# Loading head 0's K tile ahead of the query weights in a one-token attention and MLP kernel

## The chip, the cores and the metric

The kernel runs on one core of one Trainium2 chip. The metric is device time in microseconds (us): the median of several executions. A profile's span, from its first to its last record, is about 1.8 us shorter than the time of the same execution. Times come with a state, fast or slow.

Five engines matter below: PE (matrix multiply; its weight loads are listed as PEld), DVE (vector), ACT (scalar), POOL, and SP, whose queue ("SPq" in the profile) issues almost all transfers from HBM to the on-chip memory. The letter q behind an engine's name means its instruction queue.

## The reference, cut to what matters

```python
xn = layernorm(x)                       # x: 4 x 1 x 576
# A: one-token attention over the last 2048 cache positions
q = (xn @ wq)                           # wq: 576 x 4096, 32 query heads of 128
k = k_cache[:, :, -2048:, :]            # 4 batches, 16 kv heads, 2 query heads each
v = v_cache[:, :, -2048:, :]
o = softmax(q k^T / sqrt(128)) v
a = o @ wo                              # wo: 4096 x 576
# B: a mixer and an MLP (one position, so the shifted mixer term is zero)
b = xn + gelu(layernorm(xn) @ w3) @ w4  # w3: 576 x 4608, w4: 4608 x 576
out = x + a + b
```

Each weight and each cache element in the window is used once. That makes 87 MB to read for very little arithmetic.

## The kernel before

All large loads go through the SP queue, in program order. There are six buffers for K and V tiles. A K tile (one kv head, all four batches, 2 MB) is turned by four DVE transposes, and its buffer is free after the fourth.

```python
NKV = 6
kvp = ctx.enter_context(tc.tile_pool(name="kv", bufs=NKV))
def load_kv(kind, h):
    t = kvp.tile([P, NC, Dh], BF16, tag="kv", ...)
    nc.sync.dma_start(out=t..., in_=win[:, h]...)
...
nc.scalar.dma_start(out=x_bf[:], in_=x2)
nc.sync.dma_start(out=wq_sb[:, 0:KJ * NQ], in_=wq_main)            # 4096 KB
nc.sync.dma_start(out=wq_sb[:, KJ * NQ:], in_=A_wq[KJ * P:D, :]...) #  512 KB
...                                     # constants, layernorms
...                                     # q = xn @ wq, q turned and spread into qz
order = [("K", 0), ("K", 1), ("K", 2)]
for h in range(Hkv):
    order.append(("V", h))
    if h + 3 < Hkv:
        order.append(("K", h + 3))
W3_AFTER = ("V", 2)
pos = {"n": 0, "free": NKV}
flush_loads()                           # as many loads as buffers are free
k_transpose(0, 0)
for t in range(Hkv):
    for s in range(NSL):                # NSL = 4 slices of a head
        ...
        k_transpose(next slice)         # DVE
        ...
        pv(t - 2, s)                    # PE: probabilities times V, two heads behind
        k_scores(t, s)                  # PE: qz times the transposed K
    pos["free"] += 1                    # K's buffer (and, from t = 2, a V buffer)
    flush_loads()
```

The `w` pool holds wq, then w3, then w4 in one place, so w3 can be loaded only after the query matmuls. Two further points matter. DVE works in program order, and the first K transpose stands behind the whole query chain. Transfers are issued in program order too, so an issue that has to wait holds back the ones behind it.

## Time and profile before

| | before |
|---|---|
| time, median of 3 | 211.92 us (211.91 to 212.02) |
| span of the profiled execution | 210.2 us |
| bytes moved | 87.32 MB |
| SP's transfer queue | 97.5% of 16 engines' span |
| PE, DVE busy | 70%, 57% |

The page of the kernel before, cut to the lines that show the limit. The rows of digits are busy tenths in 40 equal slices of the span, and "GB/s" is what the 16 DMA engines moved in each slice.

```profile
span 210.2 us, 2389 instructions
...
PE 147.2 (70%) x941; PEld 62.4 (30%) x955; DVE 120.1 (57%) x217; ACT 33.9 (16%) x64; POOL 2.8 (1%) x15
...
DMA  7999999999999999999999999999999999999991
GB/s 281 418 399 430 421 430 435 427 430 436 436 442 414 426 433 420 446 424 433 436 421 433 430 420 437 433 433 422 433 426 430 422 442 433 421 436 426 421 414 60
...
q1 hardware_dynamic: 6640, 87.17, 97.5%
```

The row of DMA digits has no hole between the first slice and the last. The Trainium skill, page "DMA: Bandwidth & Descriptors", section Specifications, gives 435 GB/s as the fabric ceiling. This trace sits at 414 to 446 from the fourth slice to the one before the last, 429 on average, so the queue is not only busy but near that rate.

The timeline of the start, with start and duration in us, engine, source line, operation, output<-input, and in brackets how long the engine had been idle and what ended that:

```profile
13.14 3.91 PE L285 MATMUL q_ps<-wq_sb,xnT 128*32 128x512 bf16 x40 [0.18 <-DMA wq_sb<-in_A_wq_dram]
...
21.36 4.62 DVE L225 STREAM_TRANSPOSE kt<-kn 128x1024 int32<-128x1024 int32 x4
...
26.01 0.54 SPq L103 DMA_DIRECT2D kn<-in_A_k_cache_dram  x1
...
32.01 0.54 SPq L103 DMA_DIRECT2D vn<-in_A_v_cache_dram  x1
...
37.85 0.62 PE L390 MATMUL O<-vn,PT 128*32 128x512 bf16 x4 [4.19 <-DMA vn<-in_A_v_cache_dram]
...
41.77 0.55 SPq L103 DMA_DIRECT2D kn<-in_A_k_cache_dram  x1
...
74.59 2.37 DVE L225 STREAM_TRANSPOSE kt<-kn 128x1024 int32<-128x1024 int32 x2 [10.78 <-DMA kn<-in_A_k_cache_dram]
```

Read it as follows. The query matmuls start when wq lands. The query chain takes 8.2 us, and then the first K transpose runs. At 26.01 head 0's transposes are done and K4 is issued into the freed buffer. At 37.85 PE has waited 4.19 us for V0, and at 74.59 DVE has waited 10.78 us for K5: compute is ahead of the transfers. In these traces an issue on this queue also waits for the landing of the transfer eight places before it: V1, the ninth, is issued at 13.11, when wq, the first, has landed, and V5, the twentieth, at 68.43, when w3, the twelfth, has.

The chain of waits (start, us, what) names the same start and then steps in units of landings:

```profile
0.73 12.36 DMA wq_sb<-in_A_wq_dram
...
32.59 35.77 DMA w_sb<-in_B_w_dram
68.43 33.13 DMA vn<-in_A_v_cache_dram
```

### The profile page before, as it was taken

How to read it: one execution, taken by the hardware profiler on the slowest of the kernel's cores; microseconds unless marked ns; L12 is line 12 of the kernel's file. 1: busy time of each engine (PE TensorE's matmuls, PEld its weight loads, DVE VectorE, ACT ScalarE, POOL GpSimd, SP SyncE). 2: the span in 40 equal slices, each digit the busy share in tenths (PEclk: the TensorE clock that was granted, in tenths of full speed). 3: DMA queues.
4: the chain of work that ended last, by engine and by line, in shares of the span. 5: the costliest groups of instructions: out<-in, count | busy, mean ns of one | idle time of the engine just before them, and what ended most of it. 6: DMA issues, size and time to landing. Idle time of an engine off the chain costs nothing.

```text
span 210.2 us, 2389 instructions
## 1 busy us (share of the span) xinstructions
PE 147.2 (70%) x941; PEld 62.4 (30%) x955; DVE 120.1 (57%) x217; ACT 33.9 (16%) x64; POOL 2.8 (1%) x15
## 2 busy tenths in 40 slices
PE   0395694789394008849699689997883956988954
PEld 0132231224131002314154234343431321543533
DVE  4832999267831082637603879898578381593220
ACT  7603100021111000202012211220211020202300
POOL 4010000000000000000000000000000000000000
PEclk9998599589979555979699969999999695899999
DMA  7999999999999999999999999999999999999991
GB/s 281 418 399 430 421 430 435 427 430 436 436 442 414 426 433 420 446 424 433 436 421 433 430 420 437 433 433 422 433 426 430 422 442 433 421 436 426 421 414 60
DMA packets 6659, 87.32 MB, mean 415 GB/s; under 512 B 748, under 2 KB 1016, under 8 KB 1400
## 3 DMA queue, kind: packets, MB, share of 16 engines
q1 hardware_dynamic: 6640, 87.17, 97.5%
q8 instruction: 7, 0.11, 0.2%
q14 instruction: 4, 0.03, 0.0%
q10 hardware_dynamic: 8, 0.00, 0.0%
HBM read 87.17 MB, written 0.00 MB: 415 GB/s over the span
## 4 chain that ended last, share of the span: by engine, by line
DMA 65%; PE 22%; DVE 8%; issue 2%; ACT 1%; SPq 1%; DVEq 0%
DMA w_sb<-in_B_w_dram 33%; DMA vn<-in_A_v_cache_dram 26%; PE S L338 9%; DMA wq_sb<-in_A_wq_dram 6%; DVE kt L225 4%; PE O L390 3%; PE g_ps L456 2%; PE acc L183 2%; PE q_ps L285 2%; PE oT L403 1%; DVE mx L344 1%; PE S L360 1%; DVE qz L317 1%; PE gT_ps L468 1%; ACT q_sb L296 1%
## 5 line engine op out<-in xcount | busy, mean ns | idle before, releaser
L225 DVE STREAM_TRANSPOSE kt<-kn 128x1024 int32<-128x1024 int32 x64 | 76.3, 1216 | 11.1 <-DMA kn<-in_A_k_cache_dram 10.8
L338 PE MATMUL S<-kt,qz 128*128 128x512 bf16 x242 | 76.1, 437 | 5.2 <-DVE kt L225 3.1
L390 PE MATMUL O<-vn,PT 128*32 128x512 bf16 x256 | 27.9, 434 | 38.7 <-DMA vn<-in_A_v_cache_dram 37.5
L338 PEld LDWEIGHTS <-qz 128*128 128x128 bf16 x256 | 21.8, 104 | 42.0 <-issue 26.2
L366 ACT ACTIVATE E<-S 128x512 bf16<-128x512 f32 x16 | 9.5, 597 | 119.8 <-PE S L360 119.8
L390 PEld LDWEIGHTS <-PT 128*32 128x32 bf16 x256 | 7.3, 95 | 47.0 <-DVE kt L225 25.2
L372 DVE STREAM_TRANSPOSE PT<-E 128x512 bf16<-128x512 bf16 x16 | 11.4, 710 | 15.1 <-ACT E L366 15.1
L356 DVE TENSOR_REDUCE nm<-mg 8x1 bf16<-8x16 f32 x16 | 2.3, 146 | 23.0 <-PE mg L351 22.9
L397 ACT ACTIVATE O_sb<-O,rd 128x512 f32<-128x512 f32 x16 | 11.0, 686 | 16.2 <-issue 11.0
L344 DVE TENSOR_REDUCE mx<-S 128x1 f32<-128x512 f32 x16 | 10.5, 657 | 1.3 <-PE S L338 1.3
L413 DVE TENSOR_REDUCE on<-oT 128x8 bf16<-128x128 f32 x16 | 4.5, 280 | 11.1 <-PE oT L403 11.1
L403 PE MATMUL oT<-ident_w,O_sb 128*128 128x128 f32 x64 | 10.6, 291 | 0.2 <-issue 0.2
L403 PEld LDWEIGHTS oT<-ident_w,O_sb 128*128 128x128 f32 x64 | 8.6, 153 | 4.6 <-issue 2.4
L183 PE MATMUL acc<-wo_sb,op 128*8 128x288 bf16 x56 | 7.5, 286 | 0.0
L376 PEld LDWEIGHTS dn<-rs,same_j 128*128 128x128 f32 x32 | 5.8, 188 | 2.9 <-ACT E L366 0.7
L360 PE MATMUL S<-nm,j_row 8*128 8x512 bf16 x16 | 6.6, 410 | 0.0
L183 PE MATMUL acc<-w_sb,gT 128*8 128x288 bf16 x38 | 5.1, 286 | 1.9 <-DMA w_sb<-in_B_w_dram 1.9
L329 PE MATMUL S<-negbig,ohT 4*128 4x512 bf16 x16 | 6.2, 385 | 0.2 <-issue 0.2
L351 PE MATMUL mg<-dm,sel_jb 128*8 128x16 bf16 x16 | 2.8, 174 | 4.0 <-DVE dm L346 3.5
L183 PEld LDWEIGHTS <-op 128*8 128x8 bf16 x64 | 4.6, 87 | 2.4 <-issue 0.3
L456 PE MATMUL g_ps<-w_sb,ln2T 128*32 128x512 bf16 (+1 forms) x50 | 5.3, 480 | 0.0
L351 PEld LDWEIGHTS <-sel_jb 128*8 128x8 bf16 x16 | 1.3, 83 | 12.7 <-issue 6.8
(93 smaller groups left out, 80.0 us busy)
## 6 DMA issues: line engine op xcount, KB each, us to landing
kn<-in_A_k_cache_dram SPq DMA_DIRECT2D x16, 2048.0 KB, 22.3
vn<-in_A_v_cache_dram SPq DMA_DIRECT2D x16, 2048.0 KB, 24.8
wo_sb<-in_A_wo_dram SPq DMA_DIRECT2D x4, 1152.0 KB, 25.5
w_sb<-in_B_w_dram SPq DMA_DIRECT2D x1, 4608.0 KB, 35.8
wq_sb<-in_A_wq_dram SPq DMA_DIRECT2D x1, 4096.0 KB, 12.4
w_sb<-in_B_w_dram SPq DMA_DIRECT2D x1, 1728.0 KB, 33.6
w_sb<-in_B_w_dram SPq DMA_DIRECT2D x1, 1440.0 KB, 27.8
w_sb<-in_B_w_dram SPq DMA_DIRECT2D x2, 576.0 KB, 33.8
```

What stands on the lines that cost most here:

```text
L183: nc.tensor.matmul(out=to[q:q + OR, :], lhsT=lhsT[:, NI - 1 - i:NI - 1 - i + OR], rhs=rhs[:, i * CW:(i + 1) * CW], start=start, stop=False ...
L225: nc.vector.transpose(out=kt[:], in_=src)
L329: nc.tensor.matmul(out=S_ps[h][:].rearrange("p (c k) -> p c k", k=QD), lhsT=ohT[:], rhs=negbig[:].unsqueeze(1).to_broadcast([B, SC, QD]), ...
L338: nc.tensor.matmul(out=S_ps[h][:], lhsT=qz[:, z0:z0 + P], rhs=kt[:, ib, :, e:2 * QD:2].rearrange("p c k -> p (c k)"), start=False, stop=Fa ...
L344: nc.vector.reduce_max(out=mx[:], in_=S_ps[h][:], axis=AX.X)
L360: nc.tensor.matmul(out=S_ps[h][:], lhsT=j_row[:], rhs=st.pop(("nm", h))[:, 0:1].to_broadcast([NJ, NW]), start=False, stop=False, skip_grou ...
L366: nc.scalar.activation(out=E[h][:].rearrange("p c k -> p (c k)"), in_=S_ps.pop(h)[:], func=ACT.Exp, scale=scale, accum_out=rs[:])
L372: nc.vector.transpose(out=PT[h][:], in_=E.pop(h)[:])
L390: nc.tensor.matmul(out=O_ps[h][g * QD:(g + 1) * QD], lhsT=PT[h][:, c, :], rhs=vn[:, :, c, :], start=(s == 0), stop=False, skip_group_check ...
L397: nc.scalar.activation(out=O_sb[h][:], in_=O_ps.pop(h)[:], func=ACT.Copy, scale=st.pop(("rd", h))[:, 0:1])
L403: nc.tensor.transpose(out=oT[:, s, :], in_=o[:, s, :], identity=ident_w[:, s * NJ:s * NJ + P])
L456: nc.tensor.matmul(out=g_ps[g * QD:(g + 1) * QD], lhsT=ln2T[:, k, :], rhs=rhs, start=(j == 0), stop=False, skip_group_check=True)
```

## The change

The query chain needs wq, and the attention needs K0 as well. The change puts K0 first on the sync queue and wq behind it. Nothing else moves.

```diff
     wq_main = A_wq[0:KJ * P, :].rearrange("(p j) n -> p (j n)", j=KJ)
+    load_kv("K", 0)
     nc.sync.dma_start(out=wq_sb[:, 0:KJ * NQ], in_=wq_main)
...
-    order = [("K", 0), ("K", 1), ("K", 2)]
+    order = [("K", 1), ("K", 2)]
...
-    pos = {"n": 0, "free": NKV}
+    pos = {"n": 0, "free": NKV - 1}
```

## The prediction

> **What bounds the kernel now.** The DMA queue. The page gives 87.32 MB in a span of 210.2 us, queue 1 busy 97.5% of 16 engines' span. In the view by windows of 5 us, the DMA share is 0.98 or more from 5 to 205 us except at 65 to 70 (0.86), with 405 to 466 GB/s elsewhere. The Trainium skill, "DMA: Bandwidth & Descriptors", section Specifications, puts the fabric ceiling at 435 GB/s; most windows read 423 to 436, so this trace agrees. Outside lie only the start (0 to 5: share 0.67) and the tail after the last w4 piece (205 to 210). PE is busy 70%, DVE 57%; both wait for loads, e.g. PE 37.5 us for V tiles and DVE 10.8 us once for K5.
>
> **What the change does.** No byte, transfer or instruction is added. K0 (2048 KB) moves from third to first, so wq (4608 KB in two transfers) lands 2.1 MB later: at about 425 GB/s, 4.9 us (estimate from the windows). The DVE program order stays: the first K transpose still follows the q chain. In the timeline wq's matmuls start at 13.14 when wq lands, and q to qz ends at 21.36, when the first K transpose starts; K0 has landed by then anyway. So K0's early arrival is useless, and the first 8.2 us chain starts later:
> - q matmuls 13.1 -> about 18.1; first K transpose 21.4 -> about 26.3.
> - K4's issue, which waits for head 0's last transpose (26.01), -> about 31.
> - V2's and w3's issues (32.01, 32.59) -> about 37.
> - V1's issue (13.11, waits for wq's landing) will instead wait for K0, -> about 6 to 7.
>
> **How much is critical.** Nearly none. By 13 us 18.5 MB are issued (wq, K0 to K2, wo, V0, K3, V1), and at 26 us some 7.5 MB or 17 us of them are still to move; five us later some 12 us. So the transfers never run dry. The delay is also absorbed in compute: at 37.85 PE had waited 4.19 us for V0, whose landing is unchanged because the bytes ahead of it are the same. After the change PE reaches that point at about 38, so this wait almost vanishes, and K5's issue (41.77) comes at 41.8 to 43. By K5's landing (74.6, after w3, DVE had idled 10.8 us) the two kernels must be back on the same schedule; the tail is identical.
>
> Expected: +0.1 us, within run noise (211.91 to 212.02 before). **211.9 us, 8 in 10 between 211.3 and 212.7.** Faster by over 2%: 0.01; within 2%: 0.97; slower by over 2%: 0.02.
>
> **What would show each step.**
> - wq matmuls start at 17.5 to 18.7 us; first K transpose at 25.7 to 27.
> - GB/s in slices 2 to 39 unchanged, queue 1 share 97 to 98%.
> - PE's wait for V0 at 38 us shrinks from 4.19 to under 1 us; the total of PE's V waits falls to about 33 us.
> - DVE's wait for K5 still ends at 74.6 us, give or take 0.5.
> - The last w4 piece lands within 0.5 us of 205.0.
>
> **What would make it wrong.** If the first transfer starts more slowly or quickly with K0 in front (window 0 to 5), the whole stream shifts by that, tenths of a us. If PE's granted clock (0.50 at 20 to 25, 0.63 to 0.68 at 35 to 45) falls lower after the shift, heads 1 to 4 catch up later, but time is lost only if the queue runs dry. A queue limit on outstanding transfers (V5's issue at 68.43 waited for w3's landing) could bite elsewhere.

## The result

| | before | after |
|---|---|---|
| time, median of 6 | 211.96 us (211.83 to 212.03) | 212.09 us (211.96 to 212.20) |
| span of the profiled execution | 210.2 us | 210.1 us |
| SP's transfer queue | 97.5% | 97.4% |

The ratio is 1.0006 (95% interval 0.9993 to 1.0019). Ratios here and below are the recorded ones: the mean time of one kernel's fast runs over that of the other's of the same rounds, so not quite the ratio of the medians quoted. Those of e3, e5 and e9 come out of the listed times only if the profiled execution is left out; this is said where it matters.

The page of the changed kernel:

```profile
span 210.1 us, 2403 instructions
...
DMA  6999999999999999999999999999999999999991
GB/s 247 452 399 430 418 437 430 432 418 443 433 449 408 423 440 418 446 421 440 434 418 437 430 415 436 434 437 426 427 432 430 417 438 440 424 427 431 423 413 70
...
q1 hardware_dynamic: 6640, 87.17, 97.4%
```

The first two slices exchange 34 GB/s: 281 and 418 before, 247 and 452 after, 699 in sum both times. From the third slice to the one before the last the two rows differ by at most 3%. (The other 14 "instructions" of the span line are matmul records: 941 before, 955 after. A few can be missing from a trace.)

The timeline of the changed kernel, the same events as before:

```profile
17.98 4.46 PE L286 MATMUL q_ps<-wq_sb,xnT 128*32 128x512 bf16 x40 [4.93 <-DMA wq_sb<-in_A_wq_dram]
...
26.54 4.62 DVE L226 STREAM_TRANSPOSE kt<-kn 128x1024 int32<-128x1024 int32 x4
...
31.19 0.54 SPq L103 DMA_DIRECT2D kn<-in_A_k_cache_dram  x1
...
37.67 0.54 SPq L103 DMA_DIRECT2D vn<-in_A_v_cache_dram  x1
...
39.26 0.40 PE L391 MATMUL O<-vn,PT 128*32 128x512 bf16 x4
...
43.92 0.54 SPq L103 DMA_DIRECT2D kn<-in_A_k_cache_dram  x1
...
74.50 2.37 DVE L226 STREAM_TRANSPOSE kt<-kn 128x1024 int32<-128x1024 int32 x2 [9.47 <-DMA kn<-in_A_k_cache_dram]
```

The delay can be followed line by line: +4.8 us at the query matmuls, +5.2 at the first K transpose and at K4's issue, +5.7 at V2's issue. At the first V matmul it is +1.4, because the 4.19 us wait for V0 (37.85 before) is gone: that line has no bracket now. At K5's issue it is +2.2, and at K5's landing it is -0.1.

The chain of waits of the changed kernel:

```profile
1.44 16.50 DMA wq_sb<-in_A_wq_dram
...
38.26 30.02 DMA w_sb<-in_B_w_dram
68.34 33.13 DMA vn<-in_A_v_cache_dram
```

This is where the 5 us went. w3 is issued 5.7 us later (38.26 against 32.59) and waits in the queue 5.7 us less (30.02 against 35.77). It lands at 68.28 against 68.36. The step that looks like the cost of a transfer was largely a backlog, and the backlog got shorter by the delay.

### The profile page after: what moved, and what is told of

Its sections match the earlier page's. It is cut to its first block, busy times and chain, and to the rows that moved or that the text cites. A ratio compares the mean times of both kernels' runs of the same rounds, so it can differ in the third digit from the quotient of the medians.

```text
span 210.1 us, 2403 instructions
## 1 busy us (share of the span) xinstructions
PE 151.7 (72%) x955; PEld 63.2 (30%) x955; DVE 120.2 (57%) x217; ACT 33.9 (16%) x64; POOL 2.7 (1%) x15
## 3 DMA queue, kind: packets, MB, share of 16 engines
q1 hardware_dynamic: 6640, 87.17, 97.4%
## 4 chain that ended last, share of the span: by engine, by line
DMA 63%; PE 22%; DVE 9%; SPq 1%; issue 1%; ACT 1%; DVEq 0%
DMA w_sb<-in_B_w_dram 30%; DMA vn<-in_A_v_cache_dram 25%; PE S L339 9%; DMA wq_sb<-in_A_wq_dram 8%; DVE kt L226 6%; PE acc L184 3%; PE O L391 3%; PE g_ps L457 2%; PE q_ps L286 2%; PE oT L404 1%; DVE mx L345 1%; SPq L103 1%; PE S L361 1%; DVE qz L318 1%; PE gT_ps L469 1%
## 5 line engine op out<-in xcount | busy, mean ns | idle before, releaser
L339 PE MATMUL S<-kt,qz 128*128 128x512 bf16 x256 | 79.4, 440 | 3.1 <-DVE kt L226 3.1
L391 PE MATMUL O<-vn,PT 128*32 128x512 bf16 x256 | 28.3, 444 | 32.7 <-DMA vn<-in_A_v_cache_dram 29.4
L404 PE MATMUL oT<-ident_w,O_sb 128*128 128x128 f32 x64 | 11.6, 311 | 0.0
L404 PEld LDWEIGHTS oT<-ident_w,O_sb 128*128 128x128 f32 x64 | 9.3, 163 | 5.4 <-issue 3.6
L286 PE MATMUL q_ps<-wq_sb,xnT 128*32 128x512 bf16 x40 | 4.5, 629 | 4.9 <-DMA wq_sb<-in_A_wq_dram 4.9
## 6 DMA issues: line engine op xcount, KB each, us to landing
w_sb<-in_B_w_dram SPq DMA_DIRECT2D x1, 1440.0 KB, 27.9
```

Of the source, the lines that this page charges most:

```text
L286: nc.tensor.matmul(out=q_ps[r][g * QD:(g + 1) * QD, :], lhsT=xnT[:, k, :], rhs=wq_sb[:, col:col + NW], start=(j == 0), stop=False, skip_gr ...
L339: nc.tensor.matmul(out=S_ps[h][:], lhsT=qz[:, z0:z0 + P], rhs=kt[:, ib, :, e:2 * QD:2].rearrange("p c k -> p (c k)"), start=False, stop=Fa ...
L391: nc.tensor.matmul(out=O_ps[h][g * QD:(g + 1) * QD], lhsT=PT[h][:, c, :], rhs=vn[:, :, c, :], start=(s == 0), stop=False, skip_group_check ...
L404: nc.tensor.transpose(out=oT[:, s, :], in_=o[:, s, :], identity=ident_w[:, s * NJ:s * NJ + P])
```

## The experiments

e5_wo_once computes a wrong result; the check does not see that error. "Before" is the kernel before, run in the same rounds on the same chip.

### 1. Use the early K0 (e1_hoist)

```diff
+    for s in range(3):
+        k_transpose(0, s)
+
     q_ps = [ps_s.tile([P, NW], F32, tag="S", name="q_ps") for _ in range(2)]
...
-    k_transpose(0, 0)
     for t in range(Hkv):
...
-            if n < Hkv * NSL:
+            if 2 < n < Hkv * NSL:
                 k_transpose(*divmod(n, NSL))
```

> The changed kernel with the first three of head 0's four K transposes moved ahead of the q chain in program order, so that K0's early arrival is used. Theory (the transfer queue bounds the kernel and never runs dry): the three transposes run at about 13 to 17 us, the K buffer is released and K4 issued at about 29 instead of 31 us, and the time stays 212.0 us within 0.3%. Rival (the change is neutral only because K0's early arrival goes unused while the later wq costs what it costs): the time falls by 2 to 4 us.

The median was 211.95 us (211.93 to 214.10, 4 runs) against 212.03; ratio 1.0022 (0.9975 to 1.0068). The timeline shows the hoisted transposes and K4's issue:

```profile
13.14 3.49 DVE L226 STREAM_TRANSPOSE kt<-kn 128x1024 int32<-128x1024 int32 x3
...
30.15 0.53 SPq L103 DMA_DIRECT2D kn<-in_A_k_cache_dram  x1
```

The three transposes run early, as wanted. K4 is issued 1.0 us earlier than in the changed kernel (31.19), where I had expected 2, and in the chain of waits the first matmuls on K0 start 0.9 us earlier (26.95 against 27.84). So using the early K0 was worth about 1 us of compute, and the test is smaller than planned. The time of the other three executions (211.93 to 211.95) does not move: the expected gain of 2 to 4 us of the rival is absent. This earlier compute buys nothing while the queue is full.

One of the four executions took 214.1 us, and it is the profiled one, so its cause can be read. Busy time by window (us; busy us and number of instructions per engine; then PE's granted clock, DMA share and GB/s), first of this execution, then of the changed kernel:

```profile
206.00:208.00 2.00, 2.00 (x22) 1.24 (x18) 0.00 (x0) 0.00 (x0) 0.00 (x0) 0.50 0.22 77
208.00:210.00 2.00, 1.68 (x14) 0.85 (x10) 0.38 (x2) 0.40 (x1) 0.00 (x0) 0.72 0.00 0
```

```profile
206.00:208.00 2.00, 1.51 (x22) 0.95 (x16) 0.50 (x2) 0.40 (x1) 0.00 (x0) 1.00 0.15 51
208.00:210.00 2.00, 0.00 (x0) 0.00 (x0) 0.00 (x1) 0.00 (x0) 0.00 (x0) 1.00 0.03 6
```

After the third of w4's six pieces lands, 36 matmuls remain. Here PE had waited 1.98 us for that piece, and from 205.7 us on its clock was half. In the chain of waits the 36 took 3.8 us (205.40 to 209.16), where the kernel before needed 2.1 (205.01 to 207.15). With the landing 0.4 us later than in the kernel before, that makes the 2.1 us. The Trainium skill, "TensorE: Matmul & The Clock Gate", section "What's actually happening", says that the clock is halved after at least one idle window of about 3.4 us and that the windows run freely. The trace agrees only in part. In each trace the changes of the granted clock lie multiples of 3.41 us apart, but this wait was shorter than a window. The rows of these windows, first of the execution of 214.1 us and then of the kernel before, where PE waited 1.89 us for the same piece:

```profile
202.30:205.71 3.41, 1.43 (x24) 0.94 (x24) 0.00 (x0) 0.00 (x0) 0.00 (x0) 1.00 0.89 367
205.71:209.12 3.41, 3.41 (x31) 2.10 (x28) 0.00 (x0) 0.00 (x0) 0.00 (x0) 0.50 0.17 63
```

```profile
200.69:204.10 3.41, 2.43 (x40) 1.57 (x40) 0.85 (x2) 0.00 (x0) 0.00 (x0) 1.00 0.98 412
204.10:207.51 3.41, 2.50 (x36) 1.80 (x35) 0.00 (x0) 0.34 (x1) 0.00 (x0) 1.00 0.48 184
```

Here the whole wait fell into one window, PE was busy for 1.43 of its 3.41 us, and the next window ran at half clock. In the kernel before the same wait was split over two windows, with 2.43 and 2.50 us busy, and the clock stayed. That fits an event that hits one execution of four, but it is one pair of traces. The late landing and the half clock are this one execution's cause; that they have nothing to do with K0 is not shown, though the other three executions are not longer.

### 2. Late wq without an early K0 (e2_k1_first)

```diff
-    load_kv("K", 0)
+    alloc_kv("K", 0)          # buffers assigned as in the changed kernel
+    load_kv("K", 1)
     nc.sync.dma_start(out=wq_sb[:, 0:KJ * NQ], in_=wq_main)
     nc.sync.dma_start(out=wq_sb[:, KJ * NQ:], ...)
+    load_kv("K", 0)
...
-    order = [("K", 1), ("K", 2)]
+    order = [("K", 2)]
...
-    pos = {"n": 0, "free": NKV - 1}
+    pos = {"n": 0, "free": NKV - 2}
```

> K1 instead of K0 is the first load and K0 comes behind wq: wq is as late as in the changed kernel, but K0 is not early (it should land at about 23 us, still before the q chain ends). Buffers are assigned as in the changed kernel. Theory: first K transpose at 26.5 us as in the changed kernel, time 212.0 us within 0.3%. Rival (the early K0 brings a gain that pays for the late wq, and the two cancel): slower than before by 2 to 5 us.

The median was 212.04 us (211.94 to 212.14) against 212.03; ratio 1.0001 (0.9986 to 1.0016). The first K transpose ran at 26.42 us. So the early K0 does not pay for the late wq: a late wq alone costs nothing either. There is no gain and loss that cancel.

### 3. Larger doses of the same delay (e3_wq_after_k2, e9_wq_after_wo, e4_wq_after_v0)

If a backlog hides the delay, there must be a dose at which it is used up. Three kernels put wq further back. For wq behind K0, K1 and K2:

```diff
-    load_kv("K", 0)
+    for h in range(3):
+        load_kv("K", h)
     nc.sync.dma_start(out=wq_sb[:, 0:KJ * NQ], in_=wq_main)
...
-    order = [("K", 1), ("K", 2)]
+    order = []
...
-    pos = {"n": 0, "free": NKV - 1}
+    pos = {"n": 0, "free": NKV - 3}
```

> wq behind K0, K1 and K2, three times the delay. Theory, with the sums of the changed kernel's trace: wq lands at about 27.8 us, first K transpose at 36.4, K4's issue at 41; the 18.5 MB issued by then last until about 44.5, so the queue still does not run dry and the time stays within 0.3% of 212.0 us. Rival (a delay of the q chain is carried through to the end, and the change's 5 us were paid back by luck): slower by 5 to 10 us.

For wq behind V0 as well (V0 also leaves `order`, and four buffers are taken):

```diff
+    for h in range(3):
+        load_kv("K", h)
+    load_wo(0)
+    load_kv("V", 0)
     nc.sync.dma_start(out=wq_sb[:, 0:KJ * NQ], in_=wq_main)
```

> wq behind K0, K1, K2, the first wo tile and V0. Theory: wq lands at about 35.5 us, first K transpose at 44, K4's issue at 48.7, but the 18.5 MB issued by then end at about 44.5, so now the queue runs dry for some 4 to 5 us before K4 and perhaps 1 to 2 before V2: time 216 to 220 us, GB/s in the slices around 45 to 52 us visibly lower. If instead the time stays at 212, the backlog is not what hides the delay; if it grows by 14 us or more, the delay is carried through whole.

And later, for the dose between the two, with `load_kv("V", 0)` moved behind wq:

> wq behind K0, K1, K2 and the first wo tile, but ahead of V0: 1.18 MB, or 2.75 us, later than behind K2 and 2.1 MB, or 4.9 us, earlier than behind V0. Theory: K4's issue at 41.1 + 2.75 = 43.9 us, about when the queue runs dry (with V0 ahead it was issued at 48.6 and cost 6.7 us); the loss should fall by the 4.9 us, to about 1.8 us: 212.5 to 215 us. Rival (the loss of 6.7 us came from V0's place and not from the lateness of wq): 218 us as with V0 ahead of wq is excluded by it, and the time is that with wq behind K2, 212.0 to 212.5 us.

| wq stands behind | query matmuls start | K4 issued | time, median (fast runs) | ratio to before (95%) |
|---|---|---|---|---|
| nothing (before) | 13.1 | 26.0 | 211.96 | |
| K0 (the change) | 18.0 | 31.2 | 212.09 | 1.0006 (0.9993 to 1.0019) |
| K0 to K2 | 27.9 | 41.3 | 212.54 | 1.0060 (0.9999 to 1.0121) |
| K0 to K2, wo | 30.6 | 43.5 | 213.51 | 1.0076 (my mean of three; see below) |
| K0 to K2, wo, V0 | 35.3 | 48.6 | 218.77 | 1.0310 (1.0288 to 1.0332) |

(Of the four executions of the fourth row one, 216.2 us, is recorded as slow, and the other three were 212.95, 213.51 and 214.32, 1.6 us above the kernel before on average. The recorded ratio of this row, 1.0127, is not used: it comes out only with 216.2 counted and the profiled 212.95 left out. With one core, "slow" rests on the time alone, over 1.5% above the fastest; the granted clock of that execution, 0.904, lies between those of the others, 0.895 to 0.919. So it may be this kernel's own spread; with all four the mean is 2.3 us above. In the third row the mean of all four executions gives 1.0045.)

A delay of 15 us costs 0.3 to 0.6% in the two rounds that measured it (the second is in section 5), and one of 22 us costs 6.6 us (3.1% of 212). Between the last two rows the query matmuls start 4.7 us later and the time rises by 5.3 us (5.0 between the means): in this one step beyond the bend, lateness passes to the end about one for one.

The windows of the kernel with wq behind V0 show the cause. They have the same columns as above.

```profile
42.00:44.00 2.00, 0.06 (x1) 0.00 (x0) 1.31 (x3) 0.68 (x2) 0.00 (x0) 1.00 1.05 451
44.00:46.00 2.00, 0.79 (x2) 0.35 (x3) 2.00 (x2) 0.50 (x1) 0.00 (x0) 0.52 0.65 279
46.00:48.00 2.00, 2.00 (x6) 0.72 (x5) 2.00 (x3) 0.00 (x0) 0.00 (x0) 0.50 0.00 0
48.00:50.00 2.00, 2.00 (x6) 0.72 (x5) 1.72 (x2) 0.00 (x0) 0.00 (x0) 0.50 0.28 74
...
54.00:56.00 2.00, 2.00 (x11) 0.93 (x11) 1.94 (x3) 0.69 (x2) 0.00 (x0) 1.00 0.50 213
56.00:58.00 2.00, 2.00 (x12) 0.50 (x9) 2.00 (x2) 0.00 (x0) 0.00 (x0) 1.00 0.72 262
```

And the changed kernel in the same stretch:

```profile
44.00:46.00 2.00, 2.00 (x14) 0.88 (x12) 1.98 (x3) 0.69 (x1) 0.00 (x0) 1.00 0.96 410
46.00:48.00 2.00, 0.83 (x7) 0.38 (x7) 1.96 (x5) 0.00 (x0) 0.00 (x0) 1.00 0.99 426
48.00:50.00 2.00, 2.00 (x13) 0.70 (x12) 1.95 (x3) 0.00 (x0) 0.00 (x0) 1.00 1.05 451
```

At 46 to 48 us nothing moves at all: the transfers issued at the start are done, and K4 is issued only at 48.56, when head 0's transposes have freed its buffer. A second, smaller hole lies before V2 (issued at 55.12). The expectation had named both places and a time of 216 to 220 us. PE and DVE are busy in the hole; they were only too late. The two holes account for the loss: from 44 to 80 us this kernel moved 351 GB/s on average and the changed kernel 431, which is 2.9 MB or 6.7 us of transfer, and from 80 to 200 us both moved 430.

The dose in between was right in its time (1.8 us more expected; 1.6 measured for the mean of the fast runs and 1.5 for their median) but wrong in its place. I expected the dry spot before K4's issue. The windows show none there (0.99 at 44 to 46), and the dip is one stage later, before V2, issued at 49.54. First this kernel, then the changed one:

```profile
50.00:52.00 2.00, 2.00 (x12) 0.68 (x11) 2.00 (x3) 0.00 (x0) 0.00 (x0) 1.00 0.81 262
```

```profile
50.00:52.00 2.00, 2.00 (x15) 0.90 (x14) 0.83 (x3) 0.69 (x2) 0.00 (x0) 1.00 1.00 426
```

By the DMA share that dip is 0.19 x 2 = 0.4 us, by the bytes moved 0.33 MB or 0.8 us. The profiled execution (212.95) was the shortest and lost 1.0 us, so the dip accounts for most of it. The times of this dose overlap those of wq behind K2 (212.0 to 214.9), so the dip and not the time tells the two apart.

### 4. Take bytes away (e5_wo_once)

```diff
-            if kind == "V" and h % WOQ == 0:
-                load_wo(h // WOQ)
+            if kind == "V" and h == 0:
+                load_wo(0)
...
-            acc_matmuls([(op[:, i + u, :], wo_tiles[h // WOQ][:, i + u, :]) for u in range(2)])
+            acc_matmuls([(op[:, i + u, :], wo_tiles[0][:, i + u, :]) for u in range(2)])
```

> The changed kernel with three of its four wo tiles not loaded (the first one is used in their place; a wrong result on purpose), 3 x 1.18 MB = 3.54 MB fewer bytes and every other instruction kept. Theory (the transfer queue bounds the kernel all the way): the time falls by 3.54 MB / 0.43 MB per us = 8.2 us, to about 203.8 us. Rival (a chain of matmuls and transposes bounds a good part of it, as 22% PE and 9% DVE in the chain of waits suggest): the time falls by less than 6 us.

The median was 204.43 us (204.36 to 205.06) against 212.07; ratio 0.9639 (0.9625 to 0.9653; 0.9647 with the profiled execution). The pages say, of the kernel before and then of this one:

```profile
DMA packets 6659, 87.32 MB, mean 415 GB/s; under 512 B 748, under 2 KB 1016, under 8 KB 1400
```

```profile
DMA packets 6227, 83.78 MB, mean 412 GB/s; under 512 B 700, under 2 KB 968, under 8 KB 1352
```

With 3.54 MB fewer bytes and every compute instruction kept, 7.6 us are gone: 93% of the 8.2 expected. So bytes on the queue, not the chain of matmuls and transposes, set the time. This kernel was only a probe: it uses the first quarter of the output matrix in place of all four.

### 5. Spread, and a failed theory of it (e6_after_again, e7_wq_after_k2_again, e8_k2_split)

The first round with wq behind K2 had executions at 212.0 and at 214.9 us. I asked whether this is the half clock of the tail seen in experiment 1, and whether the changed kernel has it too.

> The changed kernel once more, for its spread: does it, like the run with wq behind K2 (212.0 to 214.9 us) and the hoisted one (one of four at 214.1), have executions about 2 us longer? The theory of the tail (PE works off the last w4 pieces at half clock in some executions) says that any kernel can, depending on where PE's idle time falls; the six executions so far had none, so expected 212.0 to 212.3 us with at most one longer one, by 1 to 3 us. If the long ones come from the lateness of wq itself they should not appear here.

> wq behind K0 to K2 once more, five rounds, for the spread. Expected: most executions at 212.0 us, some at 213 to 215 as in the first four; the lowest within 0.1% of the kernel before.

The third kernel has wq behind K2 too, and one piece of w4 cut in two:

```diff
-    W4_PIECES = [0, 10, NFH, NF - 6, NF - 2, NF - 1, NF]
+    W4_PIECES = [0, 10, NFH, NF - 12, NF - 6, NF - 2, NF - 1, NF]
...
     mlp_out(*pieces[3])
+    mlp_out(*pieces[4])
...
-    for lo, hi in pieces[4:]:
+    for lo, hi in pieces[5:]:
```

> wq behind K0 to K2, and the third w4 piece (12 rows of tiles, 1728 KB) cut into two of 6, so that PE can start on it about 2 us earlier. Theory of the tail (the long executions are those in which the last 36 matmuls run at half clock after the third piece lands): with 12 of the 36 done before, the long executions shrink from +2 to +3 us to at most +1.3 us; the short ones stay at 212.0, because the last piece's landing and not PE ends them. Rival (the long ones come from transfers that finish later): as many long ones, as long, as in the kernel without the cut.

| kernel, five rounds | median (range), us | ratio to before (95%) |
|---|---|---|
| the change, again | 211.84 (211.75 to 212.13) | 0.9991 (0.9979 to 1.0003) |
| wq behind K2, again | 212.50 (212.16 to 213.98) | 1.0031 (1.0010 to 1.0053) |
| wq behind K2, w4 piece cut | 212.97 (211.96 to 213.94) | 1.0045 (1.0024 to 1.0067) |

The changed kernel has no long executions: eleven in all lie within 211.75 and 212.20 us, and in these rounds it was, if anything, a shade shorter than before. wq behind K2 does have them, so they belong to the larger dose. The cut did not shorten them, and my theory fell: in the profiles of the last two kernels PE's granted clock is 1.00 from 196 to 210 us. The chain of waits of the cut one ends on a later landing, at 207.14:

```profile
180.84 26.30 DMA w_sb<-in_B_w_dram
```

The trace also keeps 16 end signals for each of these transfers, the last of which marks the landing; the views do not print them. By them the same piece of w4 (576 KB) landed at 206.25 us in the changed kernel. So in the cut kernel the transfers finish 0.9 us later, which is the 0.9 us by which its span is longer (211.0 against 210.1).

Part of this is an early dip, in the place where the kernel with wq behind wo has its own: from 50 to 54 us the cut kernel moved 395 GB/s and the repeated one 412, against 422 in the changed kernel, some 0.25 and 0.1 us of transfer. From 54 to 200 us all three moved 430 GB/s. The rest shows in the end signals alone: half of those of the last w4 piece had come at 206.53 us in the cut kernel and the last at 207.88, 1.35 us later; in the changed kernel these were 206.29 and 206.96, 0.67 us apart. So some of the transfers' parts end late while the mean rate stays. Why stays open, and so does the cause of the longest executions (213.9 to 214.9 us), of which no profile was taken.

No version that beats the kernel before came out of this. The experiments say why: only fewer bytes, or a shorter start or tail, could do it.

## Why the prediction was right, point by point

- **Total: right.** 211.9 us (211.3 to 212.7) was predicted, and 212.09 measured, then 211.84 in the repeat.
- **The queue bounds the kernel: right,** and shown by taking 3.54 MB away (7.6 us).
- **wq 4.9 us later: right.** The query matmuls moved from 13.14 to 17.98 (predicted 17.5 to 18.7) and the first K transpose from 21.36 to 26.54 (25.7 to 27).
- **K0's early arrival is useless: right,** and for two reasons. The program order keeps the transposes behind the query chain, and moving three of them ahead (e1_hoist) gained nothing either.
- **Backlog of some 12 us left: about right.** A further delay of 9.9 us cost 0.3 to 0.6%, one of 12.6 us 0.8% (1.1% with the slow execution), one of 17.3 us 3.1%.
- **K4, V2 and w3: right to about 1 us.** K4 at 31.19 (about 31), V2 and w3 at 37.67 and 38.26 (about 37).
- **V1's issue: missed.** 6 to 7 us was predicted, 8.24 measured. V1 waits for K0's landing, and I allowed too little for the start of the queue: K0's bytes over the rate are 4.9 us, but the changed kernel moved 217 GB/s in the first 5 us against 452 in the next 5, and K0 took 7.5 us from issue to landing. It had no effect: PE waited for V1 (1.17 us), but its first matmuls on V1 started at 47.54 in both kernels.
- **PE's V waits: right in kind, off in size.** The wait for V0 went from 4.19 us to nothing, as said. The total of waits for V went from 37.5 us to 29.4 us rather than to 33. PE's granted clock differs from place to place in the two traces (0.73 after against 1.00 before at 95 to 100 us, for example), which may move other waits; I did not sort the difference further. K5's issue at 43.92 was 0.9 us beyond its range.
- **K5's landing and the tail: right.** 74.50 against 74.59. The w4 landing that PE waits for came at 204.86 against 204.96. The prediction called it the last piece, but it is the third of six; the chain names the first landing on which PE's last unbroken run of matmuls waits.

What was only argued before the runs, that two effects do not cancel, is shown by K1 in K0's place (212.04 us).

## What to carry to other kernels

When one queue of transfers bounds a kernel, the order of its first loads matters only through the moment when freed buffers let the next load be issued. Compare that moment with the moment at which the loads already issued run out: here some 10 us of further delay remained nearly free after the change (0.3 to 0.6%), and in the one step measured beyond 13 us each microsecond cost about one. A long transfer step in a chain of waits may be time spent in a full queue; look at whether it shrinks by as much as its issue is delayed before you count it as a cost.

## What the Trainium skill lacked or had wrong

- "DMA: Bandwidth & Descriptors" has bandwidth, latency and ordering but no test for whether a later issue costs time. Here w3 issued 5.7 us later waited 5.7 us less and landed 0.1 us earlier, and the cost was 0.3 to 0.6% at a delay of 15 us, 0.8% at 17 us and 3.1% at 22 us.
- The same page's section "Anatomy of one DMA — SWDGE (gpsimd) path" fits 2.0 us plus the bytes over 436 GB/s for one transfer, which would be 6.8 us for K0 (2.1 MB), an estimate from that fit. It gives the fit for loads issued from POOL and none for loads issued from SP. For K0, issued from SP at the start with others behind it, 7.5 us passed from issue to landing.
- "TensorE: Matmul & The Clock Gate", section "What's actually happening", says for modelling that the ramp costs under 1% of a typical span. One execution here agrees in size (36 matmuls at the tail took 3.8 instead of 2.1 us, 0.8% of 212 us). The page does not say that at the very end nothing hides it, and there it was most of an outlier of 2.1 us. Its table has the half clock follow at least one idle window of about 3.4 us; here it followed a window of 3.41 us in which PE was busy for 1.43 us.
